# First batch pair of an attention and gated-MLP kernel: the small products C for three f tiles at a time, weight blocks converted a step sooner

## The chip, the cores and the metric

One Trainium2 chip; the kernel runs on one of its cores. The metric is device time in microseconds (us), the median over executions. TensorE is called PE, VectorE DVE, ScalarE ACT, GpSimd POOL; SP is SyncE, whose queue issues nearly all DMAs.

## The reference

Packed attention, then two MLPs. Shapes: 8 batches, 8 heads, 576 positions, head size 64, 32 packed rows; 4608 tokens of 512.

```
p_packed = softmax(p k^T / 8) v            # 32 rows per head
out      = softmax(q p_packed^T / 8) p_packed
x  = out as (4608, 512)
x  = (silu(x @ w_gate) * (x @ w_val)) @ w_out     # d_ff 1536
y  = ((x @ w1) * (x @ w2) @ w3) @ w_out           # d_ff 1024
```

The inputs of the MLP weights are float64, which the kernel turns into float32 with integer operations.

## The kernel before, in words

The second attention product is never formed by itself. With A = softmax(q p^T) (tiles aTh and aTl, a high and a low part, since every large product is made as three products of rounded parts), x @ w_gate is A @ (p_packed @ w_gate). So for each pair P of batches and each tile f of 128 columns of d_ff there is a small product **C(P, f)** = p_packed @ [w_gate, w_val] for that tile (`c_mm`, tile pc in PSUM, 16 small float32 matmuls for each half), which `c_out` splits into ch (ACT, a cast) and cl (DVE, a subtraction).

The middle of the kernel, with which the change deals, runs over `steps`: pairs P = 0 to 3, and in each f = 0 to 11. Step n of the first pair is f = n. A step does, in the order of the code (L887 to L969):

- `stage1` for both batches of the pair: pg (gate) and pv (value), 12 matmuls each, from ch, cl, aTh and aTl. ACT makes u = silu(pg), DVE u = u*pv, ACT the rounded uh, POOL the rest ul. The u of the second batch has one buffer.
- in the first pair, `w_conv`: the raw float64 blocks of w_gate and w_val (names raw_w_f_0 and raw_w_f_1) become float32 in the two halves of wf0_f. One half is an ACT operation (L349), a DVE shift into vx_w (L350) and a DVE merge (L353, called the merge below). `wo_conv` does the same for a block of w_out (wof0_f), which `wo_split` turns into woh (ACT) and wol (POOL). Each conversion starts the load of the next raw block of the list `raw_q`; there are four raw buffers. `w_store` writes wf0_f to DRAM, from where the later pairs load it.
- after each third f, `stage3`: 12 groups (px) of matmuls of u with w_out, half in the next step's first part, half in its second, accumulated by ACT or DVE in acc.
- the attention of the next pair, spread over the steps (`q_tasks`: qT transposes on DVE, psq matmuls, softmax).

Before, in the first pair, C(0, f+1) is made at the head of step f. In the later pairs three C are made together in the steps with f = 0, 3, 6, 9; there the third goes to a buffer of its own (pool cp1), while in the first pair all go to pool cp, which has two buffers for ch and two for cl.

The order of the instructions on each engine isn't that of the code: a list scheduler places them when the program is built, by its own estimates, and then each engine works through its list. `pin` and `behind` tie conversions behind a named earlier instruction: DVE's shift behind pin["dve"], ACT's operation behind pin["act"]. There are four PSUM tiles, shared by pg, pv, pc, psq and px.

Of the kernel before, what the change touches and what calls it, by code (L numbers as in the profile page):

```python
# [38 lines left out]
def packed_attention_moe_kernel(  # L39
# [35 lines left out]
    NF = DFF // 128  # L75
# [4 lines left out]
    GF = 3  # L80
# [45 lines left out]
    def psum(name):  # L126
        ps_n[0] += 1
        return ps_at[ps_n[0] % len(ps_at)].tile([128, 2, 512], F32, tag="A", name=name)
# [9 lines left out]
    in_front, conv_rest, pin, pin_at = [True], [], {}, {}  # L138
    NO_SYNC = mybir.DependencyInfo(mybir.DependencyClass.NoSync, mybir.DependencyReason.DATA)

    def behind(x, what):
        if what in pin:
            tc.add_manual_dep(x.ins, pin[what].ins.name, NO_SYNC, reason="behind the last unit")
# [19 lines left out]
    def head(b, at):  # L163
        return at ^ (b % 2)
# [121 lines left out]
    NH = NF2 // 2  # L286
    raw_q = [f"w_{f}_{gv}" for f in range(4) for gv in range(2)]
    for f in range(NF):
        if 2 <= f < NF - 2:
            raw_q += [f"w_{f + 2}_0", f"w_{f + 2}_1"]  # L290
        raw_q += [f"wo_{f}"]
    raw_q += [f"w12_{i}" for i in range(len(w12_list))]
    w3_list = []
# [42 lines left out]
    def conv(key, t):  # L336


        name, raw = raw_t.pop(0)
        assert name == key, (name, key)  # L340
        x = vc.tile(list(t.shape), I32, tag="vx", name=f"vx_{key}")
        w = raw.bitcast(I32)
        if len(t.shape) == 3:
            w = w.rearrange("p a (n e) -> p a n e", e=2)
            low, high = w[:, :, :, 0], w[:, :, :, 1]
        else:
            w = w.rearrange("p (n e) -> p n e", e=2)
            low, high = w[:, :, 0], w[:, :, 1]
        behind(nc.scalar.activation(t, high.bitcast(F32), AF.Prelu, scale=2.0 ** -112, alpha=-2.0 ** 32), "act")  # L349
        behind(nc.vector.tensor_scalar(x, low, 29, None, op0=ALU.logical_shift_right), "dve")  # L350

        def rest():
            nc.vector.scalar_tensor_tensor(  # L353
                t.bitcast(I32), t.bitcast(I32), 3, x, op0=ALU.logical_shift_left, op1=ALU.bitwise_or)

        if in_front[0]:
            conv_rest.append(rest)
        else:
            rest()
        if not in_front[0]:  # L360
            raw_load()
# [4 lines left out]
    def w_conv(f, gv):  # L366
        if gv == 0:
            wf_t[0, f] = wst_t[f] = wgv.tile([128, 4, 2, 128], F32, tag=("wh", "wl")[f % 2], name=f"wf0_{f}")
        t = wf_t[0, f]
        conv(f"w_{f}_{gv}", t[:, :, gv, :])  # L370

    def w_store(f):
        behind(nc.sync.dma_start(Wd[f], wst_t.pop(f)), "sp")
# [24 lines left out]
    def wo_split(P, f):  # L398
        hi = wop.tile([128, DM], F32R, tag="woh", name=f"woh{P}_{f}")
        lo = wop.tile([128, DM], F32R, tag="wol", name=f"wol{P}_{f}")  # L400
        split(hi, lo, wof_t.pop((P, f)), sub_on="pool")
        wo_t[P, f] = (hi, lo)

    def c_mm(P, f):
        w = wf_t.pop((P, f))
        t = psum(f"pc{P}_{f}").rearrange("p b (q n) -> p b q n", q=2)
        for Q in range(2):
            for at in range(4):
                for b in range(2):
                    hq = head(b, at)  # L410
                    es = slice(64 * (hq % 2), 64 * (hq % 2) + 64)
                    nc.tensor.matmul(  # L412
                        t[hs[at], b, Q], lhsT=PTd[es, 2 * (2 * P + b) + Q, hs[hq]],
                        rhs=w[es, 2 * Q + hq // 2].rearrange("p g n -> p (g n)"),
                        start=True, stop=True, tile_position=(64 * (hq % 2), 32 * at))
        if C_t.get("later"):
            return C_t["later"].append((P, f, t))
        c_out(P, f, t)

    def c_out(P, f, t):  # L420
        to = cp1 if P and f % GF == 0 else cp
        hi = to.tile([128, 2, 2, 256], F32R, tag="ch", name=f"ch{P}_{f}")
        lo = to.tile([128, 2, 2, 256], F32R, tag="cl", name=f"cl{P}_{f}")
        pin_at["ch"] = nc.scalar.copy(hi, t)
        pin_at["cl"] = sub(lo, t, hi)
        C_t[P, f] = (hi, lo)
# [91 lines left out]
    def pa_s(u):  # L518


        kT = kT_t.pop(u)
        t = psum(f"psp{u}")
        for hq in range(4):
            for e in range(2):
                es = slice(64 * e, 64 * e + 64)
                nc.tensor.matmul(
                    t[hs[hq], e, 0:HS].rearrange("j (m p) -> j m p", m=NR // 2), lhsT=kT[es, NR // 2, hs[hq]],
                    rhs=kT[es, 0:NR // 2, hs[hq]],
                    start=True, stop=True, tile_position=(64 * e, 32 * hq))
        mx = pa.tile([128, 1], F32, tag="mx", name=f"mx{u}")  # L530
        nc.vector.reduce_max(mx, t[:, :, 0:HS], axis=AX.XY)
        nc.vector.tensor_scalar_mul(mx, mx, -scale)
        return t, mx
# [89 lines left out]
    with tc.manual_schedule(engines=M0):  # L623
        for s in range(last + 1):
# [8 lines left out]
            if 0 <= s - 1 < U:  # L633
                x = pa_s(s - 1)
# [236 lines left out]
    def w3_task(P, f, slot):  # L871

        if P < NPR - 1 or slot not in W3S[f % GF] or f > 9 or (f == 0 and slot < 3):
            return
        i = w3_at[0]
        w3_at[0] += 1
        if 0 < i <= len(w3_list) and w3_list[i - 1].startswith("w3"):
            new = tuple(int(x) for x in w3_list[i - 1].split("_")[1:])
            w3_step(new, w3_old[0])
            w3_old[0] = new  # L880
            if new[1] == NF2 - 1:
                w3_step(None, new)
                w3_old[0] = None
        if i < len(w3_list):
            w3_conv(w3_list[i])

    for n, (P, f) in enumerate(steps):  # L887
        def at(i):
            return steps[n + i] if n + i < len(steps) else None

        if P > 0:
            wo_split(P, f)
        w3_task(P, f, 0)
        if n > 1 and at(1) is not None and n < NF:
            c_mm(*at(1))
        if n == NPS:
            psC.release()
            psA.release()
            ps = tc.alloc_tile_pool(name="ps", bufs=4, space=bass.MemoryType.PSUM, reuse_waits="tile")
            ps_at[:] = [ps]  # L900
        if (2 * P, f) not in u_t:
            stage1(2 * P, f, 0)
            stage1(2 * P, f, 1)
        if n < 4:
            w_store(n)
        if n >= 2:
            pin.clear()
        if 2 <= n < NF:
            pin.update(dve=pin_at["cl"], act=pin_at["ch"])
        if n != 1 and at(2) is not None and at(2)[0] == 0:  # L910
            for gv in range(2):
                w_conv(max(at(2)[1], 3), gv)
            if n > 1:
                w_store(at(2)[1])
        if at(4) is not None and at(4)[0] > 0:
            w_load(*at(4))
        if at(1) is not None and at(1)[0] > 0:
            wo_load(*at(1))
        w3_task(P, f, 1)
        if pend is not None:  # L920
            stage3(*pend, 0)
        w3_task(P, f, 2)
        stage1(2 * P + 1, f, 0)
        if n == 1:
            c_mm(*at(1))
        stage1(2 * P + 1, f, 1)
        if P > 0 and f % GF == 0:
            for i in range(1, GF + 1):
                if at(i) is not None:
                    c_mm(*at(i))  # L930
        if P == 0:
            wo_conv(f)
            wo_store(f)
            wo_split(P, f)
            if n >= 2:
                pin.clear()
        i = n - NF - 3
        if 0 <= i < len(w12_list):
            pin.update(pin_at)
            w12_conv(i)  # L940
            pin.clear()
        if P + 1 < NPR:
            q_tasks(2 * P + 2, 0, f)
            q_tasks(2 * P + 3, 5, f)
        if pend is not None:
            stage3(*pend, 1)
            pend = None
        C_t.pop((P, f))
        if f % GF == GF - 1:
            pend = (P, f // GF)  # L950
        if P == NPR - 1:
            if f == 0:
                aA.release()
                qp.release()
                wp = pool("wp", "left", bufs=2)
            w3_task(P, f, 3)
            if f == 9:
                assert w3_at[0] > len(w3_list)
                wp.release()
                vc.release()  # L960
                cp1.release()
                xp = pool("xp", "left", bufs=2)
                x2_prep(0, 0)
            if f == 10:
                x2_prep(0, 1)
                x2_prep(0, 2)
            if f == 11:
                x2_prep(0, 3)
                load_w12(0)  # L969
# [165 lines left out]
```

## Time and profile before

| | |
|---|---|
| median of 3 runs | 1360.7 us (1360.44 to 1363.02) |
| the profiled execution | 1364.69 us, its span 1362.6 us |
| granted TensorE clock, mean | 0.996 |
| PE busy | 1339.7 us, 98% of the span |
| DVE, ACT, POOL busy | 656.5, 570.1, 387.8 us |

The span runs from the first to the last instruction. The first pair's steps take some 150 us of it, from about 100 to 258 us. In rows of the timeline the columns are start in us, duration in us, engine, line, operation, tiles written <- tiles read, shape, and count; in brackets the idle time ahead of it and what ended it. Matmuls are pipelined: two rows' starts tell the pace, not their durations.

### The profile page before, as it was taken

What the parts mean: (1) busy time and instruction counts of PE and PEld (TensorE: products, weight loads), DVE (VectorE), ACT (ScalarE), POOL (GpSimd) and SP (SyncE); (2) the same over time, 40 slices, a digit from 0 to 9 for tenths busy, and PEclk for the clock granted to TensorE, in tenths of its full rate; (3) what the DMA queues carried; (4) which work ended last, traced back from release to release, by engine and by line L of the source; (5) the groups of instructions that cost most, each with busy time, mean ns of one, the idle gap of its engine ahead of it and who ended that gap; (6) DMA issues with size and microseconds to landing.
All of it is one profiled execution on the core that took longest, in us unless ns stands there. A gap on an engine that the chain in (4) does not pass through costs nothing.

```text
span 1362.6 us, 25518 instructions
## 1 busy us (share of the span) xinstructions
PE 1339.7 (98%) x10196; PEld 1241.7 (91%) x10196; DVE 656.5 (48%) x962; ACT 570.1 (42%) x940; POOL 387.8 (28%) x309
## 2 busy tenths in 40 slices
PE   7999999999999999999999999999999999999998
PEld 5678899999999999989999999999899899998997
DVE  3756877336564466462463379633423234234230
ACT  5774644244443454344554146423333333233331
POOL 0332322323322333243444237312112021121120
PEclk9999999999999999989999999999999999999999
DMA  9976766534545443244443249828448266285441
GB/s 318 341 222 206 209 197 200 168 77 125 151 131 183 115 120 125 71 134 132 151 142 111 65 166 338 311 89 254 160 142 254 91 211 215 88 254 162 142 145 47
DMA packets 186822, 230.27 MB, mean 169 GB/s; under 512 B 70736, under 2 KB 117840, under 8 KB 186704
## 3 DMA queue, kind: packets, MB, share of 16 engines
q1 hardware_dynamic: 186704, 228.64, 53.7%
q8 instruction: 81, 1.33, 0.4%
q14 instruction: 37, 0.30, 0.1%
HBM read 179.04 MB, written 49.55 MB: 168 GB/s over the span
## 4 chain that ended last, share of the span: by engine, by line
PE 81%; DVE 4%; DMA 1%; issue 1%; ACT 1%; SPq 0%; POOL 0%; DVEq 0%; ACTq 0%
PE px L674 19%; PE po L1072 14%; PE pA L1008 13%; PE pg L445 9%; PE pv L445 9%; PE pB L1008 6%; PE pw L766 3%; PE pC L1008 3%; PE pc L412 2%; DVE ws L89 1%; PE psq L209 1%; DMA wo3r<-wo3d 0%; DMA x2r<-X2d 0%; DVE x2T L836 0%; DMA X2d<-acc 0%
## 5 line engine op out<-in xcount | busy, mean ns | idle before, releaser
L89 POOL TENSOR_TENSOR ul<-u,uh 128x576 fp32r<-128x576 f32 x96 | 146.9, 1532 | 304.9 <-ACT uh L96 278.9
L1028 POOL TENSOR_TENSOR c<-s,s 128x384 f32<-128x384 f32 x48 | 49.2, 1024 | 375.7 <-ACT s L1023 375.5
L674 PE MATMUL px<-uh,woh 128*128 128x384 f32 x576 | 148.2, 338 | 0.2
L674 PE MATMUL px<-ul,woh 128*128 128x384 f32 x576 | 146.7, 335 | 0.0
L674 PE MATMUL px<-uh,wol 128*128 128x384 f32 x576 | 146.6, 335 | 0.0
L1023 ACT COPY s<-pA 128x384 f32<-128x384 f32 x144 | 69.0, 479 | 178.6 <-PE pA L1008 172.2
L454 DVE TENSOR_TENSOR u<-u,pv 128x576 f32<-128x576 f32 x96 | 72.0, 751 | 139.8 <-PE pv L445 126.3
L1072 PE MATMUL po<-wo_hi,abl 128*128 128x512 f32 x288 | 112.2, 390 | 0.0
L1072 PE MATMUL po<-wo_lo,abh 128*128 128x512 f32 x288 | 112.2, 390 | 0.0
L1072 PE MATMUL po<-wo_hi,abh 128*128 128x512 f32 x288 | 112.1, 389 | 0.0
L96 ACT CAST uh<-u 128x576 fp32r<-128x576 f32 x96 | 64.6, 673 | 110.7 <-DVE u L454 110.5
L674 PEld LDWEIGHTS px<-uh,woh 128*128 128x128 f32 x576 | 103.0, 189 | 6.4 <-issue 2.9
L686 DVE TENSOR_TENSOR acc<-acc,px 128x768 f32<-128x768 f32 x72 | 68.0, 948 | 81.5 <-PE px L674 81.1
L674 PEld LDWEIGHTS px<-ul,woh 128*128 128x128 f32 x576 | 104.4, 188 | 0.0
L674 PEld LDWEIGHTS px<-uh,wol 128*128 128x128 f32 x576 | 104.3, 188 | 0.0
L89 POOL TENSOR_TENSOR wol<-wof,woh 128x512 fp32r<-128x512 f32 x48 | 65.2, 1370 | 126.9 <-ACT woh L96 121.8
L89 DVE TENSOR_TENSOR abl<-ab,abh 128x768 fp32r<-128x768 f32 x48 | 49.2, 1025 | 105.3 <-ACT abh L96 105.2
L450 ACT ACTIVATE u<-pg 128x576 f32<-128x576 f32 x96 | 62.4, 650 | 88.3 <-PE pg L445 81.7
L445 PE MATMUL pg<-aTh,ch 128*128 128x288 f32 x384 | 84.3, 301 | 1.2 <-DVE cl L89 0.7
L445 PE MATMUL pv<-aTh,ch 128*128 128x288 f32 x384 | 82.9, 297 | 0.9 <-DVE cl L89 0.6
L445 PE MATMUL pg<-aTh,cl 128*128 128x288 f32 x384 | 82.4, 296 | 0.5 <-DVE cl L89 0.5
L445 PE MATMUL pg<-aTl,ch 128*128 128x288 f32 x384 | 82.6, 297 | 0.0
(308 smaller groups left out, 3093.6 us busy)
## 6 DMA issues: line engine op xcount, KB each, us to landing
ws<-wsd SPq DMA_DIRECT2D x245, 256.0 KB, 3.0
wf<-Wd SPq DMA_DIRECT2D x36, 512.0 KB, 6.4
wsd<-ws SPq DMA_DIRECT2D x49, 256.0 KB, 3.6
km<-in_k_dram SPq DMA_DIRECT2D x16, 576.0 KB, 7.8
wof<-wod SPq DMA_DIRECT2D x36, 256.0 KB, 2.9
x2r<-X2d SPq DMA_DIRECT2D x24, 384.0 KB, 5.2
out_dram<-o SPq DMA_DIRECT2D x36, 256.0 KB, 2.0
vm<-in_v_dram SPq DMA_DIRECT2D x16, 512.0 KB, 8.2
```

Source lines behind the costliest of these rows:

```text
L89: x = eng.tensor_tensor(out=out, in0=src, in1=hi.bitcast(F32), op=ALU.subtract)
L96: nc.scalar.copy(hi, src)
L445: nc.tensor.matmul(t[:, hf, 0:HS], lhsT=w[:, b % 2, Q, cols], rhs=x[:, Q, hf, :], start=first, stop=last,)
L450: x = nc.scalar.activation(u, t[:, :, 0:HS], AF.Silu)
L454: x = nc.vector.tensor_tensor(out=u, in0=u, in1=t[:, :, 0:HS], op=ALU.mult)
L674: nc.tensor.matmul(t[:, h, 0:CW], lhsT=w[:, 128 * d:128 * d + 128], rhs=x[:, CW * c:CW * c + CW], start=first, stop=last,)
L686: pin_at["acc"] = nc.vector.tensor_tensor(out=o, in0=o, in1=t[:, :, 0:CW], op=ALU.add)
L766: nc.tensor.matmul(t[:, 1], lhsT=a[:, kk], rhs=w, start=(i == 0), stop=(i == 11))
L1008: nc.tensor.matmul(bk[n], lhsT=w[:, hl, 128 * d:128 * d + 128], rhs=r[:, d], start=(first and d == 0 and i == 0), stop=(d == 1 and i == 2) ...
L1023: nc.scalar.copy(o, t)
L1028: on.tensor_tensor(out=r, in0=o, in1=t, op=op)
L1072: nc.tensor.matmul(t, lhsT=a[:, j, cols], rhs=w[:, f], start=first, stop=last)
```

## The change

In the first pair C is made for the next three f in steps 3, 6 and 9, in the middle of the step, behind the second batch's stage1; C(2) and C(3) are made in steps 1 and 2 as before. C(1, 0), the first of the second pair, comes with C(10) and C(11). `w_conv` for tile n + 3 is done in step n (before it was n + 2, but for the first), and the raw loads are listed in that order. The pins of the conversions change: in steps 3, 5, 6, 8, 9 and 11 they are tied behind the last stage1 of the step before, in steps 2, 4, 7 and 10 behind the last C.

```diff
@@ the order of the raw loads
-        if 2 <= f < NF - 2:
-            raw_q += [f"w_{f + 2}_0", f"w_{f + 2}_1"]
+        if 1 <= f < NF - 3:
+            raw_q += [f"w_{f + 3}_0", f"w_{f + 3}_1"]
...
@@ in the loop over the steps
-        if n > 1 and at(1) is not None and n < NF:
+        if n == 2:
             c_mm(*at(1))
+        start = {x: pin_at[y] for x, y in (("dve", "cl"), ("act", "ch")) if n > 1}
+        if n > 2 and n % GF != 1:
+            start = {x: pin_at[x] for x in ("dve", "act")}
...
-            pin.update(dve=pin_at["cl"], act=pin_at["ch"])
-        if n != 1 and at(2) is not None and at(2)[0] == 0:
+            pin.update(start)
+        if n < NF - 3:
             for gv in range(2):
-                w_conv(max(at(2)[1], 3), gv)
-            if n > 1:
-                w_store(at(2)[1])
+                w_conv(n + 3, gv)
+            if n > 0:
+                w_store(n + 3)
...
-        if P > 0 and f % GF == 0:
+        if n > 0 and f % GF == 0:
             for i in range(1, GF + 1):
                 if at(i) is not None:
                     c_mm(*at(i))
```

**ACT at the start of the first pair (steps 0 and 1).** In the names the numbers are batch (or pair) and f, and then a buffer; raw_w_4_1 is the second raw block of f = 4. Before:

```order
L96 CAST woh0_0_1724<-wof0_0_1716 128x512
L96 CAST woh0_1_1798<-wof0_1_1790 128x512
L450 ACTIVATE u1_0_1685<-pg1_0_1686 128x576
L96 CAST uh0_0_1454<-u1_0_1685 128x576
L450 ACTIVATE u1_1_1738<-pg1_1_1739 128x576
L424 CAST ch0_2_1770<-pc0_2_1753 128x1024
```

and now:

```order
L96 CAST woh0_0_1724<-wof0_0_1716 128x512
L349 ACTIVATE wf0_4_1738<-raw_w_4_1_1677 128x4x128
L450 ACTIVATE u1_0_1685<-pg1_0_1686 128x576
L349 ACTIVATE wof0_1_1804<-raw_wo_1_1683 128x512
L96 CAST woh0_1_1812<-wof0_1_1804 128x512
L96 CAST uh0_0_1454<-u1_0_1685 128x576
L450 ACTIVATE u1_1_1752<-pg1_1_1753 128x576
L424 CAST ch0_2_1784<-pc0_2_1767 128x1024
```

The second half of tile 4 and the w_out block of f = 1 now stand ahead of the second batch's u and of ch of C(2); before, that w_out block had been converted earlier and tile 4 came later.

**DVE at the same place.** Before:

```order
L350 TENSOR_SCALAR vx_wo_0_1717<-raw_wo_0_1396 128x512
L350 TENSOR_SCALAR vx_wo_1_1791<-raw_wo_1_1535 128x512
L353 SCALAR_TENSOR_TENSOR wof0_0_1716<-wof0_0_1716,vx_wo_0_1717 128x512
L353 SCALAR_TENSOR_TENSOR wof0_1_1790<-wof0_1_1790,vx_wo_1_1791 128x512
L454 TENSOR_TENSOR u1_0_1685<-u1_0_1685,pv1_0_1700 128x576
L89 TENSOR_TENSOR cl0_2_1771<-pc0_2_1753,ch0_2_1770 128x1024
```

and now:

```order
L353 SCALAR_TENSOR_TENSOR wf0_4_1738<-wf0_4_1738,vx_w_4_0_1739 128x4x128
L350 TENSOR_SCALAR vx_w_4_1_1745<-raw_w_4_1_1677 128x512
L353 SCALAR_TENSOR_TENSOR wf0_4_1738<-wf0_4_1738,vx_w_4_1_1745 128x4x128
L350 TENSOR_SCALAR vx_wo_1_1805<-raw_wo_1_1683 128x512
L353 SCALAR_TENSOR_TENSOR wof0_1_1804<-wof0_1_1804,vx_wo_1_1805 128x512
L454 TENSOR_TENSOR u1_0_1685<-u1_0_1685,pv1_0_1700 128x576
L89 TENSOR_TENSOR cl0_2_1785<-pc0_2_1767,ch0_2_1784 128x1024
```

Five more instructions stand ahead of the product u1_0, three of which read blocks that are the 11th and 12th of the raw loads in both versions' queue.

**PE in the middle of step 3.** Here pv1_3 is the last stage1 of the step. Before, C(5) followed the px groups of the step and C(6) the stage1 of step 4; now three C stand here:

```order
L445 MATMUL pv1_3_2081<-aTh1_1249,cl0_3_1846 128x288 x2
L412 MATMUL pc0_4_2097<-wf0_4_1738,PTd_77 32x256 x16
L412 MATMUL pc0_5_2118<-wf0_5_1883,PTd_77 32x256 x16
L412 MATMUL pc0_6_2139<-wf0_6_1989,PTd_77 32x256 x16
L209 MATMUL psq2_1_2172<-qT2_1_1952,PTd_77 32x288 x8
L674 MATMUL px0_0_3_2187<-uh0_0_1454,woh0_0_1724 128x384 x2
```

Behind the third one, which reads wf0_6, stand the psq matmuls and the px groups; before, nothing stood between pv1_3 and psq.

**DVE in the middle of step 3.** Before:

```order
L454 TENSOR_TENSOR u1_3_2073<-u1_3_2073,pv1_3_2088 128x576
L350 TENSOR_SCALAR vx_w_5_1_2003<-raw_w_5_1_1874 128x512
L216 STREAM_TRANSPOSE sT2_1926<-psq2_1_2116 128x288 x2
L353 SCALAR_TENSOR_TENSOR wf0_5_1996<-wf0_5_1996,vx_w_5_1_2003 128x4x128
L350 TENSOR_SCALAR vx_wo_3_2105<-raw_wo_3_1880 128x512
```

and now:

```order
L454 TENSOR_TENSOR u1_3_2066<-u1_3_2066,pv1_3_2081 128x576
L353 SCALAR_TENSOR_TENSOR wf0_6_1989<-wf0_6_1989,vx_w_6_0_1990 128x4x128
L160 STREAM_TRANSPOSE qT2_1_1952<-qr2_1_1819 128x576
L89 TENSOR_TENSOR cl0_4_2115<-pc0_4_2097,ch0_4_2114 128x1024
L160 STREAM_TRANSPOSE qT2_1_1952<-qr2_1_1819 128x576
L89 TENSOR_TENSOR cl0_5_2136<-pc0_5_2118,ch0_5_2135 128x1024
L350 TENSOR_SCALAR vx_w_6_1_1996<-raw_w_6_1_1888 128x512
L353 SCALAR_TENSOR_TENSOR wf0_6_1989<-wf0_6_1989,vx_w_6_1_1996 128x4x128
```

The merge that completes wf0_6 now stands behind cl of C(4) and of C(5). On ACT it is the same: its operation on raw_w_6_1 stands behind ch of C(4) and ch of C(5).

## Rows read from the trace of the kernel before

**Rows 1.** The page: each engine's busy time, share of the span, instructions.

```profile
PE 1339.7 (98%) x10196; PEld 1241.7 (91%) x10196; DVE 656.5 (48%) x962; ACT 570.1 (42%) x940; POOL 387.8 (28%) x309
```

**Rows 2.** PE's timeline in step 5: its two waits between 130 and 258 us.

```profile
154.65 0.54 PE L445 MATMUL pv<-aTh,ch 128*128 128x288 f32 x2 [0.57 <-DVE cl L89]
157.28 1.10 PE L412 MATMUL pc<-wf,PTd 64*32 64x256 f32 x32 [0.77 <-ACT uh L96]
```

**Rows 3.** PE's timeline around one C alone, then around three together.

```profile
226.74 0.51 PE L674 MATMUL px<-uh,wol 128*128 128x384 f32 x2
...
228.58 0.42 PE L445 MATMUL pg<-aTl,ch 128*128 128x288 f32 x2
...
257.82 0.42 PE L445 MATMUL pv<-aTh,cl 128*128 128x288 f32 x2
...
261.39 0.51 PE L674 MATMUL px<-ul,woh 128*128 128x384 f32 x2
```

**Rows 4.** Timeline of step 3's middle; the last row is a merge in step 5.

```profile
129.67 1.18 PE L209 MATMUL psq<-qT,PTd 64*32 64x288 f32 x16
129.85 0.76 DVE L454 TENSOR_TENSOR u<-u,pv 128x576 f32<-128x576 f32 x1 [8.79 <-PE pv L445]
130.64 0.67 ACT L96 CAST uh<-u 128x576 fp32r<-128x576 f32 x1 [1.74 <-DVE u L454]
131.22 0.67 ACT L349 ACTIVATE wf<-raw_w 128x512 f32<-128x512 f32 x1
131.39 1.43 POOL L89 TENSOR_TENSOR ul<-u,uh 128x576 fp32r<-128x576 f32 x1 [9.46 <-ACT uh L96]
131.92 1.46 DVE L353 SCALAR_TENSOR_TENSOR wf<-wf,vx_w 128x512 int32<-128x512 int32 x1 [0.15 <-ACT wf L349]
...
155.18 0.68 DVE L353 SCALAR_TENSOR_TENSOR wf<-wf,vx_w 128x512 int32<-128x512 int32 x1
```

**Rows 5.** Tile pc, all instructions: duration in ns, minimum/median/maximum.

```profile
L424 ACT CAST ch<-pc x48: 995/1014/1032, 70.6 to 764.7; 128x1024 fp32r<-128x1024 f32 x48
L89 DVE TENSOR_TENSOR cl<-pc,ch x48: 1185/1217/1232, 71.6 to 766.0; 128x1024 fp32r<-128x1024 f32 x48
```

**Rows 6.** Groups by line, 100 to 245 us: busy us, mean ns.

```profile
L160 DVE STREAM_TRANSPOSE qT<-qr 128x576 f32<-128x576 f32 x10 | 7.3, 757 | 0.6 <-DMA qr<-in_q_dram 0.6
L350 DVE TENSOR_SCALAR vx_w<-raw_w 128x512 int32<-128x512 int32 x16 | 6.1, 417 | 0.0
```

**Rows 7.** Two idle gaps of PE, and PEclk (third from last) behind each.

```profile
85.99 0.30 PE L580 MATMUL pPT<-ident,Pd 128*128 128x128 f32 x1 [1.45 <-DVE Pd L574]
86.00:88.00 2.00, 2.00 (x37) 1.59 (x37) 1.58 (x4) 1.03 (x4) 0.00 (x0) 0.58 0.86 340
88.00:90.00 2.00, 2.00 (x30) 1.74 (x23) 0.35 (x1) 2.00 (x4) 0.00 (x0) 0.57 0.84 219
599.22 3.67 PE L412 MATMUL pc<-wf,PTd 64*32 64x256 f32 x64 [2.94 <-DVE acc L686]
600.00:610.00 10.00, 10.00 (x91) 8.28 (x76) 5.56 (x6) 3.94 (x5) 1.41 (x1) 0.74 0.82 245
```

**Rows 8.** Timeline at the start of the first pair, all engines.

```profile
98.12 0.76 DVE L454 TENSOR_TENSOR u<-u,pv 128x576 f32<-128x576 f32 x1 [1.24 <-ACT u L450]
100.61 1.43 POOL L89 TENSOR_TENSOR ul<-u,uh 128x576 fp32r<-128x576 f32 x1
102.08 0.65 ACT L450 ACTIVATE u<-pg 128x576 f32<-128x576 f32 x1 [2.49 <-POOL ul L89]
103.68 0.53 PE L445 MATMUL pg<-aTh,ch 128*128 128x288 f32 x2 [0.46 <-ACT ch L424]
```

**Rows 9.** The 11th raw load: issue, time to landing; then all, 60 to 140 us.

```profile
92.87 0.39 SPq L333 DMA_DIRECT2D raw_w<-in_moe_w_gate_dram  x1
DMA to landing us min/median/max: 5.6/5.6/5.6
DMA to landing us min/median/max: 4.9/6.8/9.4
```

## The prediction

> **What bounds the kernel now.** I read the page first: PE is busy for 98% of the span [rows 1], so a time of another engine counts only where it makes PE wait. Then PE's timeline over the first pair: between 130 us and 258 us, steps 3 to 11 and the head of the second pair, PE waits twice, both times in step 5, for 0.57 and 0.77 us [rows 2]. At its start it waits 0.46 us for ch of C(2), whose PSUM tile ACT reads late [rows 8]. This bounds what the change can give back: these waits, and what it costs PE to go from one kind of matmul to the small ones of C and back. It doesn't bound what it can lose, and PE works through its list in the order that it is given, as do ACT and DVE. So I went through the new order at the places where C and the conversions have moved and put the durations of the rows on it.
>
> **Fewer changes between matmul shapes: -1.4 us.** A single C stands between a px pair that starts at 226.74 and the second pg pair at 228.58 [rows 3]. Of the 1.84 us the px pair takes 0.35 and the first pg pair 0.27, their pace where nothing interrupts; the C costs 1.22. Three together lie between 257.82 and 261.39: 3.57 - 0.27 - 0.35 = 2.95, or 0.98 each. In the order of before six of the nine moved C stand alone, three run together with psq matmuls, and I count these at 0.98 already. 6 x (1.22 - 0.98) = 1.4; the bounds are nothing and 9 x 0.24 = 2.2.
>
> **The third C of step 3 waits for its weights: +6.1 us.** Let T = 129.67 be the end of pv1_3 [rows 4]; C(4) and C(5) follow and end at T + 2.0. C(6) reads both halves of wf0_6, and the merge that completes it is behind cl of C(5) on DVE. The way there: DVE's product u1_3 ends at T + 0.9, ACT's uh at T + 1.6, its operation on the first half at T + 2.2 [rows 4]. Then DVE merges the first half, 0.68 us or 1.46, and does transpose, cl of C(4), transpose, cl of C(5), shift, merge: 0.76 + 1.22 + 0.76 + 1.22 + 0.42 + 0.68 = 5.06 [rows 4 to 6], of which some 0.08 for each of six hand-overs overlaps, 4.6. ACT's two ch of 1.01 us [rows 5] and its operation on the second half (0.67) fit in beside that: ch of C(5) ends at T + 4.1, and cl needs it at T + 5.5. The merge ends at T + 7.5 or T + 8.3, and PE has been idle since T + 2.0: 5.5 to 6.3 us. I take 6.1, since the first merge falls beside POOL's ul, as it does now (131.39 to 132.82, where the merge took 1.46; without POOL 0.68) [rows 4]. The Trainium skill (SBUF — State Buffer, section "Who interferes with whom") makes this a rule: a DVE instruction with two SBUF inputs and a GpSimd one that reads SBUF don't share, the later one is blocked whole. By it the merge is the long one and the wait 6.3; the mean of all merges alone would speak for 5.6. Nothing can hide this wait: psq and px are behind C(6) on PE. The same doesn't happen in steps 6 and 9: the last merge of wf0_9 is ahead of step 6's first accumulations, wf0_11 is whole two steps early, and C(1, 0) reads a loaded block.
>
> **The clock behind it: +2.3 us.** After an idle gap of 2.94 us PE's clock fell to the lower level, 1.2 GHz, and in the ten us from 600 the mean was 0.74: 2.6 us lost, and 0.4 before 600 [rows 7]. After a gap of 1.45 us it was 0.58 and 0.57 for two stretches of 2 us: 1.7 us lost. A gap of 6 us is longer than both. Bounds 1.7 and 3.0, middle 2.3.
>
> **The start of the pair: +2.6 us.** The second block of tile 4 is now the 11th raw load, issued at 92.87 in either version, as the queue ahead of it is the same; it landed after 5.6 us, at 98.5 [rows 9]. ACT and DVE now convert it and the w_out block behind it ahead of u1_0. ACT's operation to 99.15, the merge to 99.85, the shift of the w_out block to 100.25, its merge after ACT's operation to 101.1, then u1_0 to 101.85 instead of 98.88 [rows 8]. ACT rounds the w_out block by 101.8 and makes uh by 102.55; POOL does the rest of the w_out block, counted like its ul with 1.43, to 103.2 and ul to 104.65 instead of 102.04. u1_1 has the same buffer, so ACT starts it only then [rows 8], and ch of C(2) is behind it: pg of step 2 starts at 106.3 instead of 103.68. By the spread of the landings, 4.9 to 6.8 at the median [rows 9], the shift is 1.9 to 3.8. Behind this gap, 0.46 + 2.6 = 3.1 us and so no shorter than that of 2.94, I expect the clock to fall too: +2.3, bounds nothing (it held across 0.46 us) and 3.0. The Trainium skill (TensorE: Matmul & The Clock Gate, section "HAM oscillation — how this bites in real kernels") does not count a gap as short as this among those that bring the clock down; by it the sum would be 2.3 smaller. The gap of 2.94 in this trace speaks against that.
>
> **The waits of step 5, and later loads: +0.5 us.** The cl that PE waited for in step 5 is made in step 3 now, which gives back 0.57 + 0.77 = 1.3 [rows 2]. But the third C of each three finds both ch buffers taken: it stays in PSUM until the next step's stage1 is done, and the conversions pinned behind it (steps 4 and 7) end later, so do the loads into their raw buffers. From the end of step 4's last pv: ch, cl and a shift, 2.7 us; the load of the second block of tile 8, 4.9 to 9.4; then ACT's operation, u, DVE's product and merge, the two parts of the w_out block, 4.7: 12.3 to 16.8 us. PE comes to the px group that needs that block after four stage1 of step 5, two of step 6 (1.6 us each) and two thirds of a group (2.8): 12.4. So it waits nothing to 4.4 us; 1.8 by the median landing of 6.8. The w_out block before step 9 has the same pattern with the blocks of tile 11, and I count nothing for it. Holding one of four PSUM tiles for a step I cost at nothing: the other three turn round in two stage1, 3.2 us, in which ACT's and DVE's reads of one (0.65 and 0.76) fit; if that cover fails, a tile late by one conversion costs 0.7.
>
> **Sum.** -1.4 + 6.1 + 2.3 + 2.6 + 2.3 + 0.5 = +12.4 us. The profiled execution took 1364.7, so it would be 1377.1; it lies 4.0 us above the median of the runs, and 1360.7 + 12.4 = **1373.1 us**.
>
> **Rivals.** (A, chance 0.45) As summed, 1373.1. (B, 0.30) The clock holds across the first gap, or its loads land early: 2.3 to 3.0 less, 1370.1 to 1370.8. The two gaps of 0.46 us at that place, across which it held, speak for it. (C, 0.15) The late blocks cost their 4.4 us in step 6 and as much again in step 9 that I left out: up to 7 more, 1376 to 1380. The load that took 9.4 us speaks for it, the median against. (D, 0.04) The other side: C(6) doesn't wait, since the second half is whole when PE comes. Then only the order's gains remain if the start holds too, -1.4 - 1.3 = -2.7: 1358.0. It decides at one point, whether the last merge of wf0_6 ends before T + 2.0; the order puts cl of two C ahead of it, which is why I give it little. (E, 0.06) It waits some 2 to 3 us only, because DVE's work between the halves overlaps more than the rows tell, and the clock holds: 1360 to 1363, no change.
>
> **How the numbers follow.** 0.2% (2.7 us) is about what a measurement of this kernel tells from no change. Cases A, B and C are slower by more than that: 0.90. E is the same, 0.06; D is at the edge of faster, 0.04. The range: at the low end the smaller bounds, 5.5 + 1.7 + 1.9 - 1.4 - 1.3 = 6.4, 1367.1, and 2.1 less for a part of E: 1365.0. At the high end 6.3 + 3.0 + 3.8 + 3.0 - 1.4 - 1.3 + 4.4 = 17.8: 1378.5.
>
> **What would show it.** On PE in step 3: the third C with an idle time of 5.5 to 6.3 us ahead of it, ended by DVE's merge of wf, and a PEclk of about 0.5 behind. At the start: pg of step 2 with 3.1 us idle, ended by ACT's ch; ACT waiting for DMA ahead of the wf operation. In step 5 no wait for cl; in step 6 a px row that waits for POOL's wol. PE's shape changes show in the starts around each three C, 2.95 us. The prediction is wrong if the third C has no idle time, if the clock stays at 1.00 behind both gaps, or if the later pairs, whose order is the same, become shorter or longer.

## The result: 1.4% slower

The changed kernel takes 1380.1 us (median of 4 runs, 1378.2 to 1381.6) where the kernel before takes 1360.6: ratio 1.014, 95% interval 1.0126 to 1.0153. Run again beside later experiments it took 1382.0 (5 runs, 1377.8 to 1383.3; ratio 1.0141). The forecast was 1373.1, its range ended at 1378.5. The profiled execution took 1378.2, its span is 1376.4.

The page of the changed kernel, engine line, answers to [rows 1]: PE's work has not grown by a tenth of a microsecond, the span has by 13.8.

```profile
PE 1339.7 (97%) x10196; PEld 1241.8 (90%) x10196; DVE 661.1 (48%) x962; ACT 570.2 (41%) x940; POOL 386.2 (28%) x309
```

PE's timeline of the changed kernel, only rows with an idle time ahead of them (in brackets, with what ended it), from the front to step 9; the last row is in the last pair:

```profile
84.45 0.30 PE L580 MATMUL pPT<-ident,Pd 128*128 128x128 f32 x1 [1.45 <-DVE Pd L574]
...
103.71 0.60 PE L445 MATMUL pg<-aTh,ch 128*128 128x288 f32 x2 [3.18 <-ACT ch L424]
...
119.84 0.62 PE L674 MATMUL px<-uh,wol 128*128 128x384 f32 x2 [0.37 <-POOL wol L89]
...
138.29 1.96 PE L412 MATMUL pc<-wf,PTd 64*32 64x256 f32 x32 [6.48 <-DVE wf L353]
...
172.71 1.01 PE L674 MATMUL px<-uh,woh 128*128 128x384 f32 x2 [2.92 <-ACT woh L96]
...
174.74 1.01 PE L674 MATMUL px<-uh,wol 128*128 128x384 f32 x2 [0.39 <-POOL wol L89]
...
221.90 0.61 PE L674 MATMUL px<-uh,wol 128*128 128x384 f32 x2 [0.79 <-POOL wol L89]
...
613.83 1.96 PE L412 MATMUL pc<-wf,PTd 64*32 64x256 f32 x64 [2.94 <-DVE acc L686]
```

The start waits 3.18 us where [rows 8] have 0.46, for the same ch; the third C of step 3 waits 6.48, ended by the merge; step 5's two waits [rows 2] are gone; step 6 has a new one, 2.92 + 0.39, for the two parts of a w_out block. With 0.18 for cl behind the start gap, the first pair's waits were 0.46 + 0.46 + 0.57 + 0.77 = 2.3 us and are 14.3: +12.0.

The second part of the loss is the clock. Windows of the changed kernel from the ends of the three long waits and of the last pair's gap (the third number from the end is PEclk); the last row is a window inside the first that lies wholly at the lower clock:

```profile
103.70:108.00 4.30, 4.11 (x18) 3.77 (x19) 2.65 (x3) 2.24 (x3) 1.42 (x1) 0.60 0.99 334
138.30:142.00 3.70, 3.70 (x49) 1.65 (x50) 0.96 (x3) 0.62 (x1) 1.27 (x1) 0.56 0.91 289
172.70:180.00 7.30, 6.91 (x23) 6.40 (x24) 4.75 (x6) 1.67 (x3) 1.99 (x2) 0.56 0.88 267
613.80:620.00 6.20, 6.17 (x89) 5.45 (x90) 3.16 (x4) 3.03 (x4) 1.41 (x1) 1.00 0.76 239
104.10:107.40 3.30, 3.12 (x14) 2.77 (x13) 1.65 (x3) 1.69 (x3) 1.04 (x1) 0.50 1.02 342
```

A stretch at 0.60 that lasts 4.3 us loses 0.40 x 4.3 = 1.7; the others 1.6 and 3.2, of which 0.2 were idle anyway: 6.3 us. The fourth shows the gap of [rows 7] again, 2.94 us, but this time the clock held, and so it did behind the gap of 1.45. The profile of before lost 1.7 and 3.0 us at these two places. From the second pair on the order is that of before on every engine. What differs there, which gaps cost clock and the waits of the second MLP (0.63 us in before, 1.53 here, 0.30 in the repeat), differs between runs of one kernel too.

The same windows of the repeated changed kernel, whose waits are the same to 0.2 us but for 0.70 in place of 0.39:

```profile
106.00:114.00 8.00, 8.00 (x38) 7.72 (x39) 5.54 (x7) 2.91 (x4) 1.42 (x1) 0.61 0.78 273
141.70:148.00 6.30, 6.29 (x60) 4.01 (x61) 3.29 (x6) 0.62 (x1) 1.26 (x1) 0.63 0.97 300
176.70:184.00 7.30, 6.58 (x20) 6.07 (x21) 4.78 (x6) 1.68 (x3) 2.01 (x2) 0.53 0.89 264
618.20:622.00 3.80, 3.76 (x67) 2.12 (x68) 2.15 (x3) 2.50 (x3) 1.41 (x1) 0.65 0.71 191
```

Here it lost 3.1, 2.3, 3.1 and 1.3: 9.8 us.

One stretch shows how the two parts add up: from pg of step 2 to the second px pair behind the three C of the second pair's first step, which starts at 261.39 in [rows 3]. In the changed kernel, then in its repeat:

```profile
275.96 0.51 PE L674 MATMUL px<-ul,woh 128*128 128x384 f32 x2
```

```profile
105.99 0.85 PE L445 MATMUL pg<-aTh,ch 128*128 128x288 f32 x2 [3.18 <-ACT ch L424]
...
280.38 0.51 PE L674 MATMUL px<-ul,woh 128*128 128x384 f32 x2
```

Before, it takes 261.39 - 103.68 = 157.7 us; now it takes 172.2 and, in the repeat, 174.4: 14.5 and 16.7 more. Waits are 9.3 of it (9.4 in the repeat), the clock 6.3 (8.5); that is 1.1 (1.3) more than the difference, which is what the fewer shape changes give back. With the 2.7 us that the start waits longer ahead of the stretch, the repeat's 16.7 make 19.4, and the medians differ by 19.5. In the first profile the start costs nothing on balance (103.71 against 103.68), as the profile of before lost 1.7 us of clock ahead of it, and what follows the stretch is 0.8 shorter.

Over nine runs the changed kernel's mean granted clock is 0.990 to 0.994, that of before in its runs beside these 0.996 to 1.000. So one profiled execution doesn't tell the clock's share; several do.

### The profile page after: what moved, and what is told of

Read it like the earlier page. It is cut to its first block, busy times and chain, and to the rows that moved or that the text cites. A ratio compares the mean times of both kernels' runs of the same rounds, so it can differ in the third digit from the quotient of the medians.

```text
span 1376.4 us, 25506 instructions
## 1 busy us (share of the span) xinstructions
PE 1339.7 (97%) x10196; PEld 1241.8 (90%) x10196; DVE 661.1 (48%) x962; ACT 570.2 (41%) x940; POOL 386.2 (28%) x309
## 4 chain that ended last, share of the span: by engine, by line
PE 85%; DMA 5%; DVE 5%; ACT 2%; issue 2%; POOL 1%; SPq 0%; DVEq 0%; ACTq 0%; POOLq 0%
PE px L674 20%; PE pA L1011 14%; PE po L1075 14%; PE pg L445 10%; PE pv L445 9%; PE pB L1011 7%; PE pC L1011 3%; PE pw L766 3%; PE pc L412 2%; DMA raw_w<-in_moe_w_val_dram 1%; DMA km<-in_k_dram 1%; DMA vr<-in_v_dram 1%; PE psq L209 1%; DMA qr<-in_q_dram 1%; DVE wf L353 1%
```

## Experiments

The theory: waits of 12 us, minus 1.4 for fewer shape changes, and the clock behind three of the waits, at the lower of its two levels (1.2 GHz, PEclk 0.50), makes up the rest of 1380.1 - 1360.6 = 19.5. The rivals: a wait taken away only moves; step 6's wait is a load, not the buffer; the clock isn't part of it. All edits are against the changed kernel unless said, all ratios against the kernel before on the same chip.

**The third C of step 3 at the end of its step.**

```
-            for i in range(1, GF + 1):
+            for i in range(1, GF if n == 3 else GF + 1):
...
+        if n == 3:
+            c_mm(*at(GF))
```

> Step 3 computes only C(4) and C(5) in its middle; C(6) goes to the end of the step, behind the second half of the queries' scores and the three px groups. Median of the changed kernel: 1380.1 us. My theory: TensorE's wait of 6.48 us in step 3 is one wait, for the merged block wf_6 that is not ready yet, and the half clock behind it costs 1.5 us more; both go, so 1380.1 - 6.5 - 1.5 = 1372.1 us (1370.5 to 1374.5); the waits of step 6 (2.92 + 0.39) stay, because C(6) still has to wait for a buffer of C(4). Rival: the wait only moves, the px groups or the scores then wait for the same conversions on VectorE and ScalarE: 1378 to 1381 us.

Measured: 1377.4 us, 1.0120 (1.0106 to 1.0133), 2.7 less instead of 8. PE's timeline:

```profile
135.56 0.68 PE L209 MATMUL psq<-qT,PTd 64*32 64x288 f32 x4 [2.54 <-DVE qT L160]
...
171.41 1.01 PE L674 MATMUL px<-uh,woh 128*128 128x384 f32 x2 [3.09 <-ACT woh L96]
```

The expectation failed in the main: of the 6.48 us 2.54 stay, since the queries' scores, now next on PE, need a transpose that stands in the same DVE queue among merge and cl; a half clock follows it too. That step 6 keeps its wait came as said.

**A buffer of its own for the third C's copies.**

```
-        to = cp1 if P and f % GF == 0 else cp
+        to = cp1 if (P or not in_front[0]) and f % GF == 0 else cp
```

> The third C of each group (6 and 9) is copied out of PSUM into a buffer of its own in the first pair too, so that its ch and cl need not wait until both halves of C(4) are used. My theory: the late ch and cl of C(6) push the conversions of tile 7 and 8 and with them woh of step 6; with the buffer the waits of step 6 (2.92 + 0.39 us), the half clock behind them (3.1 us) and the wait of step 9 (0.79) go: 1380.1 - 7.2 = 1372.9 us (1371 to 1376); the 6.48 us of step 3 stay. Rival: step 6 waits because the raw blocks arrive late or GpSimd and ScalarE are full, whatever the buffer: 1379 to 1381 us, with the waits of step 6 still in the trace.

Measured: 1372.3 us, 1.0081 (1.0067 to 1.0094): 7.8 less, as the theory said (7.2). The waits of steps 6 and 9 are gone from the timeline, the 6.47 of step 3 stay. ACT's timeline of the two kernels, first the changed one, then this one, shows the cause: ch of C(6).

```profile
157.97 1.02 ACT L424 CAST ch<-pc 128x1024 fp32r<-128x1024 f32 x1
...
169.85 0.67 ACT L349 ACTIVATE wof<-raw_wo 128x512 f32<-128x512 f32 x1
...
172.03 0.62 ACT L96 CAST woh<-wof 128x512 fp32r<-128x512 f32 x1 [0.48 <-DVE wof L353]
```

```profile
140.75 1.01 ACT L424 CAST ch<-pc 128x1024 fp32r<-128x1024 f32 x1 [0.33 <-PE pc L412]
...
159.06 0.66 ACT L349 ACTIVATE wof<-raw_wo 128x512 f32<-128x512 f32 x1
...
165.55 0.61 ACT L96 CAST woh<-wof 128x512 fp32r<-128x512 f32 x1
```

In the changed kernel it is made only when step 4's stage1 has used up C(4); with it 17 us earlier, the conversions behind it let woh of step 6 end 6.5 us earlier.

**Tiles 4 and 5 both converted in step 2, none in step 1.**

```
-        if n < NF - 3:
+        for x in ([4, 5] if n == 2 else [n + 3] if n != 1 and n < NF - 3 else []):
             for gv in range(2):
-                w_conv(n + 3, gv)
+                w_conv(x, gv)
```

> Step 1 converts no tile, step 2 converts tiles 4 and 5 (the raw blocks come in that order too); steps 3 and later are as in the changed kernel. My theory: the start gap of TensorE (3.18 us, for ch of C(2)) goes back to below 1 us, and the half clock behind it (1.9 us) goes too: 1380.1 - 2.4 - 1.9 = 1375.8 us (1374 to 1378). Rival: the two tiles are only late in step 2 instead, in front of C(4) and the ul of step 2, and TensorE waits there for as long: 1379 to 1382 us.

Measured: 1374.7 us, 1.0096 (1.0082 to 1.0110), 5.4 less. PE's timeline:

```profile
101.07 0.53 PE L445 MATMUL pg<-aTh,ch 128*128 128x288 f32 x2 [0.45 <-ACT ch L424]
...
122.37 0.53 PE L445 MATMUL pv<-aTh,ch 128*128 128x288 f32 x2 [0.80 <-ACT u L450]
125.15 1.10 PE L412 MATMUL pc<-wf,PTd 64*32 64x256 f32 x32 [0.92 <-DVE u L454]
128.68 1.96 PE L412 MATMUL pc<-wf,PTd 64*32 64x256 f32 x32 [2.43 <-DVE cl L89]
136.63 1.10 PE L412 MATMUL pc<-wf,PTd 64*32 64x256 f32 x32 [1.11 <-DVE wf L353]
```

The start gap goes back to 0.45, which shows that its cause is tile 4's conversion. Step 3's one wait becomes four, 5.3 us in sum.

**Conversions a step sooner, C for one tile at a time.** The places of C and the pins as before:

```
-        if n == 2:
+        if n > 1 and at(1) is not None and n < NF:
             c_mm(*at(1))
...
-        if n > 0 and f % GF == 0:
+        if P > 0 and f % GF == 0:
```

> The weight blocks are converted a step sooner as in the changed kernel, but C is computed for one tile per step as before, with the pins of before: the conversion part of the change alone. My theory: what the conversion part costs is the start gap and its clock (2.4 + 1.9 us); the waits of steps 3 and 6 belong to the grouping and do not appear: 1360.6 + 4.3 + 1.4 (the C alone costs its shape changes again, as before, so nothing more) = about 1365 us (1362.5 to 1367). Rival: conversions a step sooner cost the later steps as well (step 6 waits for woh because more is converted ahead of it): 1369 to 1374 us. If the start gap is not from the conversions at all: 1360 to 1361.5 us.

Measured: 1369.8 us, 1.0062 (1.0048 to 1.0076), 8.6 above before on that chip. The size is the rival's, the place is not: step 6 doesn't wait, but the start does, and step 3, by the timeline:

```profile
103.23 0.54 PE L445 MATMUL pg<-aTh,ch 128*128 128x288 f32 x2 [3.19 <-ACT ch L424]
...
132.27 0.68 PE L209 MATMUL psq<-qT,PTd 64*32 64x288 f32 x4 [1.70 <-ACT uh L96]
...
814.53 0.41 PE L1009 MATMUL pA<-xB11h,ws 128*128 128x384 f32 x1 [2.37 <-DVE acc L686]
```

The third row, behind the last pair, is 0.63 us in before and at most 1.05 in the other kernels but one; why it grew I didn't follow, and some 1.7 of the 8.6 us lie there, not in the conversions. The waits of steps 6 and 9 come with the grouping, and so does most of step 3's (1.70 us are left of 6.48, for another tile).

**Step 3's wait filled with work.** C(5) is computed six more times into the third C's PSUM tile, which C(6) then overwrites; no result changes.

```
-        for Q in range(2):
+        fill = [last_w[0]] * 6 if (P, f) == (0, 6) else []
+        last_w[0] = w
+        for ww in fill + [w]:
+          for Q in range(2):
```

> In step 3 TensorE computes C(5) six more times into the PSUM tile of C(6) before C(6) itself, which overwrites it: work that fills the wait of 6.48 us (six times 0.98 us) and changes no result. Median of the changed kernel: 1380.1 us. My theory: the wait for wf_6 ends as before, but the clock does not fall behind it, and the 1.5 to 2.4 us that the profiles of the changed kernel and of the one with the buffer of its own lost there come back: 1378.1 us (1377 to 1379.3). Rival: the clock behind the wait costs nothing that the end sees, or the repeats run late and hold C(6) up: 1380 to 1383 us.

Measured: 1378.2 us, 1.0121 (1.0102 to 1.0139): 2.0 less in the median, but its runs spread from 1376.0 to 1380.7, so by the times alone this is not settled. The profile shows the point: C(6) starts 8.46 us after C(4), as without the filling (8.44), and PEclk over step 3 is 1.00.

```profile
138.78 1.10 PE L416 MATMUL pc<-wf,PTd 64*32 64x256 f32 x32 [1.06 <-DVE wf L353]
```

```profile
132.00:148.00 16.00, 14.94 (x298) 12.22 (x278) 11.11 (x14) 7.96 (x10) 2.72 (x2) 1.00 0.66 178
```

**All three long waits filled.** As above, and C(3) three times more before the start's wait, the px group's products with its first w_out block three times more in step 6.

```
+        fill = {(0, 3): [w] * 3, (0, 6): [last_w[0]] * 6}.get((P, f), [])
...
-        for n in ns:
-            f = GF * g + n
+        for n in [-GF] * 3 * ((P, g, j, 0) == (0, 1, 0, ns[0])) + list(ns):
+            f = GF * g + n % GF
```

> The changed kernel with TensorE's three long waits filled by work that changes no result: C(3) three times more before its wait at the start, C(5) six times more in step 3, the products with the first w_out block of the px group three times more in step 6. Median of the changed kernel: 1380.1 us. My theory: about half of what the change costs is the clock that falls behind these waits; with TensorE busy in them 1.9 + 1.5 to 2.4 + 3.1 us come back: 1373 us (1372 to 1375.5). Rival: the waits alone are the cost, or the clock falls at other places instead: 1378 us and above.

Measured: 1372.6 us, 1.0079 (1.0064 to 1.0093): 7.6 less than the first runs of the changed kernel, 9.5 less than its repeat on the same chip, with nine C and one px group's worth of products more on PE. The mean clock of its six runs is 0.998 or 0.999. Windows over the three places:

```profile
102.00:112.00 10.00, 8.91 (x128) 7.71 (x112) 7.12 (x11) 6.07 (x10) 2.40 (x2) 1.00 0.95 288
132.00:148.00 16.00, 16.00 (x260) 14.22 (x244) 10.79 (x14) 6.60 (x9) 1.43 (x2) 1.00 0.61 155
166.00:178.00 12.00, 11.49 (x68) 11.00 (x68) 9.42 (x13) 3.60 (x6) 4.76 (x4) 1.00 0.98 325
```

Not all of the gain is the clock. With the filling the scheduler ordered step 3 another way: both merges of wf_6 now stand ahead of cl of C(4), and the nine C from C(4) to C(6) run without a gap:

```profile
128.97 8.03 PE L416 MATMUL pc<-wf,PTd 64*32 64x256 f32 x288
131.25 1.45 DVE L353 SCALAR_TENSOR_TENSOR wf<-wf,vx_w 128x512 int32<-128x512 int32 x1 [0.39 <-ACT wf L349]
132.62 1.21 DVE L89 TENSOR_TENSOR cl<-pc,ch 128x1024 fp32r<-128x1024 f32 x1
```

Over the stretch used above (104.60 to 269.50 here) it is 9.5 us shorter than the repeat, of which the repeat's half clock is 8.5; the other 1.0 is waits that are longer than the work that fills them. So the clock's share of the 19.5 us is some 6 to 8.5, the 6.3 and 8.5 of the two profiles.

**The changed kernel repeated.**

> The changed kernel once more, beside the filled one. Both theories: 1378 to 1381.5 us; the profile tells whether the half clock stands behind the same three waits as in the first one.

Measured: 1382.0 us, half a microsecond above the expectation; the half clock stands behind the same three waits, and behind the last pair's gap as well (windows above).

**Third C late, buffer and later start together.**

> Third C late, buffer of its own, and tiles 4 and 5 converted in step 2, all three together. If their gains add as measured alone (2.7, 7.8 and 5.4 us of 1380.1): 1364.2 us (1362.5 to 1366). Rival: the late third C and the later start serve the same wait of step 3, since with tiles 4 and 5 in step 2 that step waits in four places (5.26 us in sum) whatever C(6) does: 1366.5 to 1370 us.

Measured: 1367.9 us, 1.0038 (1.0025 to 1.0052), the rival: the gains don't add. The waits of 0.80, 0.92 and 2.42 us in step 3 are those of the kernel with the later start, and one of 1.35 for ul is new in step 6.

**The merges of tile 6 ahead of the copies.** With the buffer; a list remembers each block's two operations, and in step 3 the conversions are pinned to nothing:

```
+        if (P, f) in ((0, 4), (0, 5)):
+            for x, y in zip((pin_at["ch"], pin_at["cl"]), conv_at["w_6_1"]):
+                tc.add_manual_dep(x.ins, y.ins.name, NO_SYNC, reason="behind the third block")
...
-        if n < 4:
-            w_store(n)
+        for x in {0: [0, 1], 1: [2, 3]}.get(n, []):
+            w_store(x)
```

> With the buffer of its own (median 1372.3 us), and in step 3 the two merges of tile 6 stand ahead of cl of C(4) and C(5) on VectorE, its ScalarE operations ahead of their ch; the stores of tiles 0 to 3 go out one or two steps sooner, since the buffer of tile 2 is the one that tile 6 takes. The work is the same, only its order differs. My theory: TensorE's 6.47 us are the place in the queues, not the amount of work; the first merge falls into VectorE's idle 11 us, the second ends about 1.6 us after C(5): 4.9 us of the wait and 1.5 to 2.4 us of clock go: 1365.5 us (1364.5 to 1368). Rival: the amount of work of step 3 sets the end, and scores or px groups wait instead (as behind the late third C, where 2.54 us stayed and 2.7 of 8 us were gained): 1369.5 to 1373 us.

Measured: 1368.1 us, 1.0046 (1.0032 to 1.0061), 4.2 less than with the buffer alone (on another chip; by the ratios 4.8) where 6.8 were expected. The wait is 2.30 in place of 6.47 (1.6 expected), and the px group now waits 0.86 + 0.40 for its w_out block:

```profile
138.24 1.96 PE L413 MATMUL pc<-wf,PTd 64*32 64x256 f32 x32 [2.30 <-DVE wf L354]
```

So most of the wait was the place in DVE's queue, as the theory had it; the rest moved.

**The same with tiles 4 and 5 in step 2.**

> As the merge-first kernel, and tiles 4 and 5 both converted in step 2, none in step 1. If the start's gain is as it was alone (5.4 us, or 2.4 of wait and 1.9 of clock) and adds to the merge-first kernel's forecast of 1365.5: 1360.5 us (1359.5 to 1363), level with the kernel before. Rival: step 3 then has its waits again in other places (2.43 for cl, 1.11 for wf, 0.92 and 0.80 in the kernel with the start back): 1364 to 1369 us.

Measured: 1372.2 us, 1.0076 (1.0061 to 1.0090), worse than either forecast. The start is at 0.45, but psq now waits 0.72 + 1.16 for transposes, stage1 and C 0.80 + 0.92, and a px group 2.82 for its w_out block, with half a clock behind it; 2.29 us more of waiting fall behind the last pair, outside the change. With two tiles' conversions in step 2, TensorE waited in step 2 or 3 in all three orders tried (this one and the two above).

**The kernel before up to step 5, the change from there.** Against before: tiles 6 and 7 converted in step 4, each later one a step sooner than before; three C in steps 6 and 9, with the buffer.

```
+    conv_at = {0: [3], 2: [4], 3: [5], 4: [6, 7], 5: [8], 6: [9], 7: [10], 8: [11]}
...
-        if P > 0 and f % GF == 0:
+        if n > 5 and f % GF == 0:
```

> The kernel before, up to C(6) in step 5; from there on as the change has it, with the buffer of its own: tiles 7 to 11 converted sooner (two in step 4), C for three tiles at once in steps 6 and 9. My theory: the costs lie in the first four steps, where TensorE stands close behind the conversions, and in the shared buffer; without them the change is worth what its shape changes are, 1.4 us less, and step 5's waits stay: 1359.5 us where the kernel before is 1361 (1358.5 to 1361.5), hardly to be told from no change. Rival: conversions a step sooner cost wherever they stand: 1364 us and above.

Measured: 1364.3 us, 1.0021 (1.0009 to 1.0032; 12 runs), 3.0 above before, which is the rival's size. Its profiled execution took 1361.7, and its timeline has only two waits more than 0.5 us between 102 us and the last pair, 0.98 for cl and 1.54 for ul, 1.2 more than before's two; the shape changes give back at most 1.4. So the waits and shapes of one profile balance near nothing where the runs show 3 us. Much of the rest is clock: the mean granted clock of its 12 runs is 0.9970, that of the 17 runs of before 0.9984, which is 0.14% or some 1.8 us; behind which gaps it falls more often, one profile doesn't tell.

## Why the prediction was wrong

**Fewer shape changes, -1.4: right.** Three C of step 6 lie in the changed kernel, as in [rows 3], 3.57 us from the last pv to the second px pair (186.20 to 189.77). Over the whole stretch above, 1.1 and 1.3 us are given back.

**Third C of step 3, +6.1: right.** 6.48, 0.2 above the upper bound, ended by DVE's merge of wf; the first merge took 1.42 beside POOL's ul, as [rows 4] had it. The Trainium skill's rule in "Who interferes with whom" (SBUF — State Buffer) gave 6.3 and was the nearer bound. In steps 6 and 9 the third C doesn't wait, as said.

**The start, +2.6: right in size, partly by luck in its cause.** 3.18 us in place of 0.46, ended by ch; counting the shorter wait for cl behind it, +2.4. ACT and DVE did wait for the load, and u1_1 for POOL, as said. But the bounds came from the spread of the landings, and the landing didn't set the wait. In the five profiles with this order of the start (the changed kernel twice, the late third C, the buffer alone, C for one tile at a time) the load took 5.2 to 5.7 us, and the wait was 3.18 or 3.19 in each. DVE's shift of the block, for which the sum has no term, took 1.05 to 1.54 us beside POOL's wol, where [rows 6] have 0.42, and ended some 0.3 behind it. In the changed kernel:

```profile
95.19 1.29 POOL L89 TENSOR_TENSOR wol<-wof,woh 128x512 fp32r<-128x512 f32 x1
...
95.66 1.12 DVE L350 TENSOR_SCALAR vx_w<-raw_w 128x512 int32<-128x512 int32 x1 [1.71 <-DMA raw_w<-in_moe_w_val_dram]
```

The load was issued at 89.94, not at the 92.87 of before's profile: that one had lost clock ahead of it. PE came earlier by about as much, so the error cancelled.

**The clock behind these two, 2.3 + 2.3: right.** It fell behind both: 1.7 + 1.6 = 3.3 us in the first profile, 3.1 + 2.3 = 5.4 in the second, on either side of the 4.6.

**The waits of step 5, and later loads, +0.5: this term failed, by its size.** The chain began as said: ch of C(6) late, the conversions pinned behind it, 2.7 us from step 4's last pv to the shift that frees the raw buffer; and step 5's 1.3 came back. But step 6 waits 3.3 us, not 1.8 (0 to 4.4 were the bounds), and steps 2 and 9 wait 0.37 and 0.79, for which I counted nothing: +3.1. The load, counted at 6.8 and feared at 9.4, was not the cause: it took 3.8, to 164.48. What failed is the 4.7 us counted from its landing to the two parts of the w_out block: they took 10.2, to 174.69. DVE is busy for all of 163.3 to 172.0 (8.70 us: DVE is the third engine in the window row), and the shift of that block and two merges take 1.23 to 1.51 us beside POOL's ul and wol, where [rows 4] and [rows 6] have 0.68 and 0.42. The load of tile 8's second block, then DVE, in the changed kernel:

```profile
160.64 0.39 SPq L333 DMA_DIRECT2D raw_w<-in_moe_w_val_dram  x1
DMA to landing us min/median/max: 3.8/3.8/3.8
163.30:172.00 8.70, 6.49 (x45) 6.18 (x43) 8.70 (x14) 4.54 (x8) 4.95 (x4) 1.00 1.01 351
165.91 1.24 DVE L353 SCALAR_TENSOR_TENSOR wf<-wf,vx_w 128x512 int32<-128x512 int32 x1
167.07 1.51 DVE L350 TENSOR_SCALAR vx_w<-raw_w 128x512 int32<-128x512 int32 x1
...
170.77 1.23 DVE L353 SCALAR_TENSOR_TENSOR wof<-wof,vx_wo 128x512 int32<-128x512 int32 x1
```

And I asked at two gaps whether the clock falls and not at this third one, which came out as long as the one in [rows 7]: 3.0 us in the first profile, 3.1 in the second. The term is 6.1 in place of 0.5, 5.6 of the 7.0 us by which the median was missed; the buffer alone took 7.8 away. The other 1.4 lie within the spread of the clock between runs: the two clock terms above differ by 2.1 us between the two profiles. Rival C had steps 6 and 9 costing more and came nearest (1376 to 1380; chance 0.15), but without the clock.

**Against the profiled execution the sum looks better than it was.** Forecast 1377.1, measured 1378.2: only 1.1 short. The profile of before lost 4.7 us of clock behind the two gaps of [rows 7], which goes far to explain why it lies 4.0 above its median (other runs of before have a mean clock of 1.000 and spans of 1356 to 1358); that of the changed kernel lost nothing there. The two accidents hid most of the missing 5.6. That the changed kernel's profile would stand 4.0 above its median as well was wrong: it is the fastest of its first four runs.

No version tried is faster than the kernel before. What the change can give back is some 1.2 + 1.3 us, the shape changes and step 5's waits; its conversions in steps 1 to 3 cost more than that in every kernel that keeps them.

## What to carry to other kernels

A buffer pair that holds for one product at a time does not hold for three: look at who still reads the first when the third is to be copied, and at what is queued behind that copy. Price every new wait of TensorE twice, its length and the half clock behind it, and compare a profiled execution with the median only after taking from it what its own gaps cost in clock. A step that moves work earlier is bounded by the queue it is moved into: undoing one wait in steps 1 to 3 brought out the next.

## What was not expected of the hardware

Whether the clock falls behind a gap differs from run to run at the same place. The last pair's gap of 2.94 us (2.94 to 3.30 in 13 profiles) lowered it in 9 of them and not in 4; the front's gap of 1.45 us in 5 and not in 8. The 3.1 to 3.2 us at the start lowered it in all 7 profiles that have them. The Trainium skill (TensorE: Matmul & The Clock Gate, section "HAM oscillation — how this bites in real kernels") doesn't count gaps as short as these among those that bring the clock down; these runs don't agree with it.
